# Scores moved behind the turned attention weights, between the first and second pair of key rows, in a one-core attention and channel-mix kernel

## The chip, the cores and the metric

One core of a Trainium2 chip. The metric is the device time of one execution in microseconds (us); the kernel before takes 578.88 us, the median of three runs (578.82 to 579.36). Below, PE is the matrix engine (TensorE), DVE the vector engine, ACT the scalar engine, SP the engine whose queue issues nearly all DMAs.

## The reference

Attention inside chunks of 64 tokens, per batch (8) and head (8), then a channel mix over 512 channels in which each token also sees its predecessor:

```python
scores = q_c @ k_c^T / sqrt(64)              # chunks of 64 tokens, head size 64
attn   = softmax(scores);  x = attn @ v_c     # heads side by side: 8 x 576 x 512
xk = mu_k * x + (1 - mu_k) * x_prev;  xr = mu_r * x + (1 - mu_r) * x_prev
k  = relu(xk @ w_k) ** 2                      # 512 -> 1024
out = sigmoid(xr @ w_r) * (k @ w_v)           # 1024 -> 512
```

All in float32. The large products run as three float32r matmuls over a high and a low part of each operand.

## The kernel before, in words

The 4608 tokens are 18 groups of 256. After a start-up (table `START`), the loop `group(g)` writes one **period** for each of the groups 2 to 17. A period holds the channel mix of group g and the attention of the next groups. Its order is written out by hand in the string `GROUP` (line 56): `K1.0` is step 0 of task `K` with index 1 in this period; a first character is a condition on g from `WHEN` (line 1294); a step that a line names a second time has been issued already and is skipped. Each engine runs its own instructions in the order in which the words stand. In a period PE does:

- `K0` to `K3` (`moe_k`, line 636): four pairs of key rows, 24 matmuls of 256 columns each, into `pk`. ACT takes each out of PSUM (relu, square).
- `Pq.0` (`group_turned`, line 1078): 8 transposes of the normalised attention weights of group g+1 into `pt`, behind `K0`. Step `Pq.1` copies `pt` to SBUF on ACT.
- `R0`, `R1` (`moe_r`, line 689): 24 matmuls of 512 columns into `pr`; ACT's sigmoid (line 703) takes each out.
- `Pq.2` (line 1096): attention times v into `xps`, 32 small products on 64x64 quarters of the array (each shows as two matmuls), then `Nn.0` (`group_scores`, line 1010): the scores of group g+2 into `s`, in the same form. Only the scores read `qT` and `kT`.
- `W` (`moe_halves`, line 909): seven products of 12 matmuls of 256 columns. The first goes to `vx` (called X), the second to `vyz` (called Z). `W.16` is DVE's last step on X, W.3 to W.14 are other steps of DVE and ACT on these results.

On DVE, `De` (`turn`, line 386) turns 256 tokens of q and k from a ring in SBUF into `qT` and `kT`, `Lm` loads the next half ring (32 DMAs on SP), `Lv` loads v for the next products (8 DMAs on SP). `Sn` is the softmax of group g+2 (max, subtract, exp on ACT, sum, reciprocal, normalise = `Sn.6`), `Mr` the mix for `R` (mix on DVE, high part on ACT, low part on DVE).

PSUM is four pools: `ps_s` (one buffer, shared in turn by `s` and `pt`), `ps_x` (one buffer, `xps` and `vyz` in turn), `ps_k` (two, `pk`), `ps_o` (two, `pr` and `vx` in turn). So X waits for the sigmoid of the first `pr`, and Z for ACT's copy of `xps` (line 1122).

Of the kernel before, what the change touches and what calls it, by code (L numbers as in the profile page):

```python
# [7 lines left out]
F32 = mybir.dt.float32  # L8
# [3 lines left out]
AF = mybir.ActivationFunctionType  # L12
# [4 lines left out]
P = 128  # L17
CH = 64
TT = 128
# [34 lines left out]


GROUP = """
=Nc.0 K0.0 =L4 <Sc.0 <Sc.1 K0.12 >Pq.0 >Pq.1 Mr.0 De.01 Lm <Sc.2 K0.3 B.01 K0.4 K1.0 K1.12 E.0 Mr.1 <Sc.3456 Mr.2 K1.34 K2.0 K2.12 E.1 H.0 K2.34 B.23
K3.0 <Pq.0 K3.12 Z.0 <Pq.1 K3.34 Z.1 H.1 H.3 Z.2 H.4 Z.3 H.2 H.5 Z.456
R0.0 R1.0 Pq.2 +Nn.0 Lv Z.78 R0.1 R1.1 Pq.3 Pq.4 C.0 B.4567 C.2 Md.0 Mk.0 B.8 C.4
V0 V1.0 W.0 W.1 W.2 !W.3 !W.4 W.5 W.6 W.7 Mk.1 W.8 W.9 *Sn.0 *Sn.1 W.10 *Sn.2 Mk.2 =Dl.01 C.1 C.3 V1.12345678 C.5 *Sn.3456 W.12 W.11 ~W.3 ~W.4 W.13 W.14 W.15 W.16 =Nn.0  # L60
"""


# [18 lines left out]
def tile_chunk_attention_channel_mix(  # L82
# [12 lines left out]
    nc = tc.nc  # L95
    B_, H, S, D = q.shape
    DM, FF = w_k.shape
    w_k, w_v, w_r = (w.bitcast(I32) for w in (w_k, w_v, w_r))
    HP = H // 2
# [3 lines left out]
    NG = B_ * S // G  # L103
# [19 lines left out]
    ps_s = ctx.enter_context(tc.tile_pool(name="ps_s", bufs=1, space=PSUM))  # L123
    ps_x = ctx.enter_context(tc.tile_pool(name="ps_x", bufs=1, space=PSUM))
    ps_k = ctx.enter_context(tc.tile_pool(name="ps_k", bufs=2, space=PSUM))
    ps_o = ctx.enter_context(tc.tile_pool(name="ps_o", bufs=2, space=PSUM))

    do = Steps()
    T = {}
# [36 lines left out]
    HB = NBLK // 2  # L166
# [96 lines left out]
    B = {}  # L263
# [191 lines left out]
    def x_tile(g):  # L455
        return xp.tile([P, NB, G + 4], F32, tag="x", name=f"x_{g}")
# [527 lines left out]

    def group_scores(g):

        b0, b1 = 8 * g, 8 * g + 8
        late = HB * 4 if g == 4 else b1
        for part, (first, last) in enumerate(((b0, late), (late, b1))):
            do.task = f"D{g}{'el'[part]}"
            for nm in "qk":
                if first < last:
                    do(lambda _, nm=nm, first=first, last=last: turn(nm, first, last - first), "D")

        do.task = f"N{g}"  # L1000

        def f_s(_):
            T[f"s{g}"] = ps_s.tile([P, 2, 2, HP, CH], F32, tag="s", name=f"s_{g}")
            back = -1 if g > SPLIT else 1
            for tl in (0, 1)[::back]:
                for hp in range(HP):
                    for e in (0, 1)[::back]:
                        cols = slice(tl * TT + e * CH, tl * TT + (e + 1) * CH)
                        for j in range(2):
                            nc.tensor.matmul(  # L1010
                                T[f"s{g}"][halves[e], j, tl, hp, :],
                                qT[halves[j], hp, cols],
                                kT[halves[j], hp, cols],
                                start=True,
                                stop=True,
                            )

        do(f_s, "P")

    def load_period(m):  # L1020

        return max(2, (HB * m - 10) // 8 - 2)

    def group_attention(g):
        do.task = f"S{g}c"
# [45 lines left out]
    def group_turned(g):  # L1071
        do.task = f"P{g}q"

        def f_tr(_):
            T[f"pt{g}"] = ps_s.tile([P, 2, HP, TT], F32, tag="s", name=f"pt_{g}")
            for tl in range(2):
                for hp in range(HP):
                    nc.tensor.transpose(  # L1078
                        out=T[f"pt{g}"][:, tl, hp, :],
                        in_=T[f"pg{g}"][:, tl, 2 * hp : 2 * hp + 2, :],  # L1080
                        identity=ident,
                    )

        def f_pT(_):
            T[f"pTg{g}"] = att.tile([P, 2, HP, TT], F32, tag="p", name=f"pT_{g}", bufs=1)
            nc.scalar.activation(T[f"pTg{g}"], T[f"pt{g}"], AF.Copy)

        def f_pv(_):
            T[f"xps{g}"] = ps_x.tile([P, NB, G], F32, tag="x", name=f"xps_{g}")
            for tl in range(2):  # L1090
                for a in range(HP // 2):
                    for e in range(2):
                        for c in range(2):
                            for j in range(2):
                                hp = 2 * a + c
                                nc.tensor.matmul(  # L1096
                                    T[f"xps{g}"][
                                        halves[c], 2 * j + a, tl * TT + e * CH : tl * TT + (e + 1) * CH
                                    ],
                                    T[f"v{2 * g + tl}"][halves[j], hp, e, :],  # L1100
                                    T[f"pTg{g}"][halves[j], tl, hp, halves[e]],
                                    start=True,
                                    stop=True,
                                )

        def f_open(_):
            x = T[f"xg{g}"] = x_tile(g)
            if g * G % S == 0:
                nc.vector.memset(x[:, :, 0:1], 0.0)
            elif g == 3:  # L1110
                seg = x_cuts(2 * g - 1)[-1]
                last = seg[2] + seg[1]
                nc.vector.tensor_copy(out=x[:, :, 0:1], in_=xt[2 * g - 1][:, :, last : last + 1])
            else:
                s, n, c = group_cuts(g - 1)[-1]
                nc.vector.tensor_copy(out=x[:, :, 0:1], in_=T[f"xg{g - 1}"][:, :, c + n : c + n + 1])
            for s, n, c in group_cuts(g)[1:]:
                nc.vector.memset(x[:, :, c : c + 1], 0.0)

        def f_x(_):  # L1120
            for s, n, c in group_cuts(g):
                nc.scalar.activation(
                    T[f"xg{g}"][:, :, c + 1 : c + 1 + n], T[f"xps{g}"][:, :, s : s + n], AF.Copy
                )

        do(f_tr, "P")
        do(f_pT, "A")
        do(f_pv, "P")
        do(f_open, "D")
        do(f_x, "A")  # L1130
# [69 lines left out]
    for t in range(6):  # L1200
# [5 lines left out]
        if t in (1, 3):  # L1206
            g = t // 2
# [12 lines left out]
    with tc.manual_schedule():  # L1220
        for word in START.split():
            name, _, e = word.partition(":")
# [8 lines left out]

    def group(g):
        now = [m for m in range(4, 2 * B_) if load_period(m) == g]
        for m in now:
            load_blocks(f"m{m}", HB * m, HB)
        if g == 2:
            group_scores(3)
            for nm in "qk":
                del do.steps[f"D3e.{'qk'.index(nm)}"]
        if g + 2 < NG:  # L1240
            for t in (2 * g + 4, 2 * g + 5):
                load_v(t)
            group_scores(g + 2)
        for n in {2: (3,), 3: (4,), 4: (5, 6)}.get(g, (g + 2,)):
            if n < NG:
                group_attention(n)
        if g + 1 < NG:
            group_turned(g + 1)
            group_mix(g + 1)
        for fp in range(NF // 2):  # L1250
            moe_k(g, fp)
        for tl in range(2):
            moe_r(g, tl)
        split_weights(g)
        if g < SPLIT:
            for tl in range(2):
                moe_v(g, (tl,))
        else:
            moe_halves(g)
        steps = late | do.take()  # L1260
        late.clear()
        late.update({k: v for k, v in steps.items() if k.startswith(f"M{g + 1}r")})
        for k in late:
            del steps[k]
        names_of = {
            "L4": ["bqm4", "bkm4"],
            "Lm": [f"b{nm}m{m}" for m in now for nm in "qk"],
            "Lv": [f"v{2 * g + 4}", f"v{2 * g + 5}"],
            "De": [f"D{g + 2}e"],
            "Dl": [f"D{g + 2}l"],  # L1270
            "Nc": [f"N{g + 1}"],
            "Nn": [f"N{g + 2}"],
            "Sc": [f"S{g + 1}c"],
            "Sn": [f"S{g + 2}c"],
            "Pq": [f"P{g + 1}q"],
            "Md": [f"M{g + 1}d"],
            "Mk": [f"M{g + 1}k"],
            "Mr": [f"M{g}r"],
        }
        for word in GROUP.split():  # L1280
            when = WHEN.get(word[0])
            if when:
                if not when(g):
                    continue
                word = word[1:]
            task, _, numbers = word.partition(".")
            for name in names_of.get(task, [f"{task[0]}{g}{task[1:]}"]):
                which = [numbers] if task == "W" else numbers
                for i in which or range(NF + 1):
                    if f"{name}.{i}" in steps:  # L1290
                        fn, e = steps.pop(f"{name}.{i}")
                        fn(e)
        assert not steps, steps.keys()
# [1 line left out]
    WHEN = {  # L1295
        "=": lambda g: g == 2,
        "+": lambda g: g > 2,
        "*": lambda g: g >= 4,
        "<": lambda g: g < 5,
        ">": lambda g: g >= 5,  # L1300
        "!": lambda g: g == NG - 1,
# [34 lines left out]
```

## Time and profile before

| what | before |
|---|---|
| time, median of 3 runs | 578.88 us (578.82 to 579.36) |
| the profiled execution's own time | 577.52 us |
| its span, first to last instruction | 575.7 us |
| PE busy | 566.3 us, 98% |
| DVE busy | 460.1 us, 80% |
| ACT busy | 362.4 us, 63% |
| one period, from `K0` to the next `K0` | 29.42 us |

The span is what the trace covers; the time is 1.8 us more, work around the program. The median of the runs is 1.36 us above the profiled execution. A busy PE is not a PE at its peak, since matmuls overlap: the time is read from the distance between starts, which the chain of work gives.

### The profile page before, as it was taken

To read this page: it belongs to the slowest core of one execution; us is meant where nothing else is said; L and a number is where in the kernel's file an instruction comes from. 1 tells how busy PE (TensorE), PEld (TensorE's weight loads), DVE (VectorE), ACT (ScalarE), POOL (GpSimd) and SP (SyncE) were. 2 spreads that over 40 slices of the span, in tenths; PEclk is the share of its full clock that TensorE was granted. 3 is DMA by queue.
4 is the path that set the end of the run, shared out by engine and by line. 5 is a ranking of instruction groups with operands and counts; after the bars stand their busy time and mean duration, and the time that the engine had idled before them with its cause. 6 is when DMAs were issued, how large, how long until landed. Compare 5 with 4: busy or idle time off the path is not lost.

```text
span 575.7 us, 15315 instructions
## 1 busy us (share of the span) xinstructions
PE 566.3 (98%) x6485; PEld 538.5 (94%) x6485; DVE 460.1 (80%) x763; ACT 362.4 (63%) x535; POOL 0.7 (0%) x6
## 2 busy tenths in 40 slices
PE   8899999999999999999999999999999999999997
PEld 7779999999999999999999999999999999999997
DVE  2799898899978969796969696979697969795744
ACT  4898974473747574748484747474747575666461
POOL 0000000000000000000000000000000000000000
PEclk9999999999999999999999999999999999999999
DMA  9997342443544343430233424343433311111011
GB/s 288 207 319 193 97 72 75 94 70 64 107 107 66 88 67 92 65 93 11 63 64 77 86 56 93 66 86 72 89 70 81 73 42 38 38 39 38 1 38 38
DMA packets 184276, 49.25 MB, mean 86 GB/s; under 512 B 169608, under 2 KB 176272, under 8 KB 184208
## 3 DMA queue, kind: packets, MB, share of 16 engines
q1 hardware_dynamic: 183904, 48.01, 37.0%
q8 instruction: 51, 0.84, 0.6%
q10 hardware_dynamic: 304, 0.27, 0.1%
q14 instruction: 17, 0.14, 0.1%
HBM read 38.80 MB, written 9.44 MB: 84 GB/s over the span
## 4 chain that ended last, share of the span: by engine, by line
PE 94%; DMA 2%; DVE 1%; SPq 1%; ACT 1%; issue 0%
PE pk L636 35%; PE pr L689 17%; PE vx L909 15%; PE vyz L909 11%; PE pv L720 6%; PE xps L1096 3%; PE s L1010 2%; DMA wr_st<-in_moe_w_r 2%; PE pt L1078 2%; PE mxk L580 1%; PE mxr L580 1%; SPq L186 1%; PE xps L494 0%; PE s L410 0%; PE pt L474 0%; DVE m L422 0%
## 5 line engine op out<-in xcount | busy, mean ns | idle before, releaser
L636 PE MATMUL pk<-xkhi,wk 128*128 128x256 f32 x1152 | 208.7, 281 | 0.0
L636 PEld LDWEIGHTS pk<-xkhi,wk 128*128 128x128 f32 x1152 | 179.0, 189 | 0.3
L636 PE MATMUL pk<-xklo,wk 128*128 128x256 f32 x576 | 161.3, 280 | 0.0
L636 PEld LDWEIGHTS pk<-xklo,wk 128*128 128x128 f32 x576 | 108.3, 188 | 0.1
L656 ACT ACTIVATE rr<-pk 128x512 f32<-128x512 f32 x60 | 35.8, 597 | 115.2 <-PE pk L636 115.2
L689 PE MATMUL pr<-wr,xrhi 128*128 128x512 f32 x288 | 89.5, 392 | 0.0
L909 PE MATMUL vyz<-b,kk 128*128 128x256 f32 x540 | 68.9, 277 | 0.0
L909 PE MATMUL vx<-b,ks 128*128 128x256 f32 x540 | 68.9, 277 | 0.0
L909 PEld LDWEIGHTS vx<-b,ks 128*128 128x128 f32 x540 | 64.9, 188 | 0.0
L909 PEld LDWEIGHTS vyz<-b,kk 128*128 128x128 f32 x540 | 64.8, 188 | 0.0
L689 PEld LDWEIGHTS pr<-wr,xrhi 128*128 128x128 f32 x288 | 52.8, 188 | 10.1
L689 PE MATMUL pr<-wr,xrlo 128*128 128x512 f32 x144 | 56.1, 389 | 0.0
L855 DVE TENSOR_TENSOR ss<-rr 128x512 f32<-128x512 f32 x15 | 10.4, 693 | 46.0 <-ACT rr L663 46.0
L938 ACT ACTIVATE u<-vx 128x256 f32<-128x256 f32 x30 | 11.5, 384 | 51.5 <-PE vx L909 51.5
L663 ACT ACTIVATE rr<-rr 128x512 f32<-128x512 f32 x60 | 37.9, 632 | 1.9
L747 DVE TENSOR_TENSOR kk<-rr,kk 128x1024 fp32r<-128x1024 f32 x30 | 35.4, 1222 | 2.9 <-ACT kk L893 1.6
L720 PE MATMUL pv<-b,kk 128*128 128x256 f32 x288 | 33.9, 277 | 0.0
L720 PEld LDWEIGHTS pv<-b,kk 128*128 128x128 f32 x288 | 33.1, 188 | 0.1
L689 PEld LDWEIGHTS pr<-wr,xrlo 128*128 128x128 f32 x144 | 27.0, 188 | 5.8
L747 DVE TENSOR_TENSOR xrlo<-mr,xrhi 128x1024 fp32r<-128x1024 f32 x15 | 18.4, 1225 | 15.4 <-ACT xrhi L1168 15.4
L747 DVE TENSOR_TENSOR ks<-ss,ks 128x512 fp32r<-128x512 f32 x45 | 28.3, 684 | 0.0
L1158 DVE SCALAR_TENSOR_TENSOR mk<-d,mu,x 128x256 f32<-128x256 f32 (+3 forms) x80 | 27.7, 413 | 0.4
(130 smaller groups left out, 882.0 us busy)
## 6 DMA issues: line engine op xcount, KB each, us to landing
v<-in_v SPq DMA_DIRECT2D x144, 64.0 KB, 2.4
out<-sg SPq DMA_DIRECT2D x34, 256.0 KB, 2.3
q_ring<-in_q SPq DMA_DIRECT2D x192, 36.0 KB, 2.0
k_ring<-in_k SPq DMA_DIRECT2D x192, 36.0 KB, 2.1
wk_st<-in_moe_w_k SPq DMA_DIRECT2D x4, 1024.0 KB, 11.7
wv_st<-in_moe_w_v SPq DMA_DIRECT2D x4, 1024.0 KB, 7.7
wr_st<-in_moe_w_r SPq DMA_DIRECT2D x2, 1024.0 KB, 10.3
q_ring<-in_q SPq DMA_DIRECT2D x2, 512.0 KB, 6.7
```

What stands on the lines that cost most here:

```text
L580: nc.tensor.matmul(m[:, cb, s : s + w], diag[nm, n][:, cb], x[:, cb, c0 : c0 + w], start=(n == 0), stop=(n == 1),)
L636: nc.tensor.matmul(pk[:, e, :], wk[a][:, cb, f * P : (f + 1) * P], xk[b][:, cb, :], start=(n == 0), stop=(n == 3 * NB - 1),)
L656: nc.scalar.activation(r, T[f"pk{g}{fp}"], AF.Relu)
L663: nc.scalar.activation(r, r, AF.Square)
L689: nc.tensor.matmul(pr, xr[a][:, cb, tl * TT : (tl + 1) * TT], wr[b][:, cb, :], start=(n == 0), stop=(n == 3 * NB - 1),)
L720: nc.tensor.matmul(T[f"pv{g}{tl}"][:, cols[c]], kk[a][:, f, tok[tl]], quarter(f // HF, c)[:, b, f % HF, :], start=(f == 0 and n == 0 and c ...
L747: nc.vector.tensor_tensor(to, x, y, ALU.subtract)
L909: nc.tensor.matmul(to, a[i][:, f, :], weight(w, j, f), start=first and f == 0 and n == 0, stop=f == HF - 1 and n == 2, skip_group_check=True,)
L1010: nc.tensor.matmul(T[f"s{g}"][halves[e], j, tl, hp, :], qT[halves[j], hp, cols], kT[halves[j], hp, cols], start=True, stop=True,)
L1078: nc.tensor.transpose(out=T[f"pt{g}"][:, tl, hp, :], in_=T[f"pg{g}"][:, tl, 2 * hp : 2 * hp + 2, :], identity=ident,)
L1096: nc.tensor.matmul(T[f"xps{g}"][halves[c], 2 * j + a, tl * TT + e * CH : tl * TT + (e + 1) * CH], T[f"v{2 * g + tl}"][halves[j], hp, e, :] ...
L1158: nc.vector.scalar_tensor_tensor(out=to[:, cb, s : s + w], in0=T[f"d{g}"][:, cb, s : s + w], scalar=mu[:, cb : cb + 1], in1=T[f"xg{g}"][:, ...
```

## The change

For the scores of group n, formed in period n-2:

- Periods 6 to 15: the scores stand directly behind the transposes `Pq.0`, between `K0` and `K1`. In period 5 they stand between `K2` and `K3`. In periods 2 to 4 nothing changes.
- From period 5 on, `pt` is two tiles in `ps_o` and no longer one in `ps_s`. The copy `pT` on ACT becomes two instructions of 128x512 (in all periods).
- q and k are turned three periods ahead and not two, from group 8 on (`turn_period`). Period 5 turns groups 7 and 8, and loads two half rings. `De` stands ahead of `Mr.0` from period 5 on.
- On DVE, `W.16` (X taken out) moves ahead of the normalising step `Sn.6` in periods 4 to 16. The products on PE keep their order.

```diff
-=Nc.0 K0.0 =L4 <Sc.0 <Sc.1 K0.12 >Pq.0 >Pq.1 Mr.0 De.01 Lm <Sc.2 K0.3 B.01 K0.4 K1.0 K1.12 E.0 Mr.1 ...
+=Nc.0 K0.0 >Pq.0 $Nn.0 =L4 <Sc.0 <Sc.1 K0.12 >Pq.1 >De.01 Mr.0 De.01 #K1.0 #K2.0 #Nn.0 ^Lm <Sc.2 K0.3 B.01 K0.4 K1.0 K1.12 E.0 Mr.1 <Sc.3456 Mr.2 #D8.01 #Lm K1.34 ...
-R0.0 R1.0 Pq.2 +Nn.0 Lv ...
+R0.0 R1.0 Pq.2 %Nn.0 Lv ...
-... C.5 *Sn.3456 W.12 W.11 ~W.3 ~W.4 W.13 W.14 W.15 W.16 =Nn.0
+... C.5 *Sn.345 W.12 W.15 *W.16 *Sn.6 W.11 ~W.3 ~W.4 W.13 W.14 W.16 =Nn.0
...
-        return max(2, (HB * m - 10) // 8 - 2)
+        return max(2, turn_period((HB * m - 10) // 8))
+    def turn_period(g):
+        return g - 2 if g < 8 else g - 3
...
-            T[f"pt{g}"] = ps_s.tile([P, 2, HP, TT], F32, tag="s", name=f"pt_{g}")
+            if g < 6:
+                x = ps_s.tile([P, 2, HP, TT], F32, tag="s", name=f"pt_{g}")
+                T[f"pt{g}"] = [x[:, tl] for tl in range(2)]
+            else:
+                T[f"pt{g}"] = [ps_o.tile([P, HP, TT], F32, tag="o", name=f"pt{tl}_{g}") for tl in range(2)]
...
-            nc.scalar.activation(T[f"pTg{g}"], T[f"pt{g}"], AF.Copy)
+            for tl in range(2):
+                nc.scalar.activation(T[f"pTg{g}"][:, tl], T[f"pt{g}"][tl], AF.Copy)
...
-            "De": [f"D{g + 2}e"],
+            "De": [f"D{g + 2 if g < 6 else g + 3}e"],
+            "D8": ["D8e"],
...
-        "*": lambda g: g >= 4,
+        "*": lambda g: 4 <= g < NG - 1,
+        "%": lambda g: 3 <= g < 5,
+        "#": lambda g: g == 5,
+        "^": lambda g: g != 5,
+        "$": lambda g: g >= 6,
```

PE in period 8, before: the last matmul of `K0`, the transposes, the first of `K1`; further on the last of `R1`, `xps`, the scores of group 10, and the first of X.

```order
L636 MATMUL pk_8_0_3990<-xkhi_8_3871,wk1_119 128x256
L1078 MATMUL pt_9_4018<-ident_109,p_9_3948 128x128 x8
L636 MATMUL pk_8_1_4070<-xkhi_8_3871,wk0_118 128x256
...
L689 MATMUL pr_8_1_4186<-wr0_120,xrlo_8_4030 128x512
L1096 MATMUL xps_9_4199<-pT_9_4027,v_18_3850 64x64 x16
L1096 MATMUL xps_9_4199<-pT_9_4027,v_19_3855 64x64 x16
L1010 MATMUL s_10_4232<-kT_123,qT_122 64x64 x32
L909 MATMUL vx_8_4293<-b11_978,kk0_8_4126 128x256 x2
```

The same places of the changed kernel:

```order
L636 MATMUL pk_8_0_4033<-xkhi_8_3914,wk1_119 128x256
L1085 MATMUL pt0_9_4058<-ident_109,p_9_3991 128x128 x4
L1085 MATMUL pt1_9_4059<-ident_109,p_9_3991 128x128 x4
L1007 MATMUL s_10_4068<-kT_123,qT_122 64x64 x32
L636 MATMUL pk_8_1_4150<-xkhi_8_3914,wk0_118 128x256
...
L689 MATMUL pr_8_1_4266<-wr0_120,xrlo_8_4112 128x512
L1104 MATMUL xps_9_4279<-pT_9_4104,v_18_3893 64x64 x16
L1104 MATMUL xps_9_4279<-pT_9_4104,v_19_3898 64x64 x16
L909 MATMUL vx_8_4340<-b11_978,kk0_8_4206 128x256 x2
```

One run of 64x64 work in a period has become two, and X stands directly behind `xps`.

DVE at the turn from period 8 to 9, before: the softmax sums of group 10 (`z`), the normalising step, six steps on the products of group 8, then the mix `mr`, the turn of q and k, and the low part of `xr`.

```order
L1057 RECIPROCAL z_10_4368<-z_10_4368 128x16
L1061 TENSOR_TENSOR p_10_4363<-p_10_4363,z_10_4368 128x1024
L952 TENSOR_TENSOR sg_8_1_4279<-u1_8_4308,sg_8_1_4279 128x256
...
L952 TENSOR_TENSOR sg_8_0_4277<-vx_8_4293,sg_8_0_4277 128x256
L1158 SCALAR_TENSOR_TENSOR mr_9_4446<-d_9_4284,mu2_115,x_9_4281 128x256 x4
L386 STREAM_TRANSPOSE qT_122<-q_ring_116 128x4x64
...
L747 TENSOR_TENSOR xrlo_9_4445<-mr_9_4446,xrhi_9_4444 128x1024
```

And in the changed kernel:

```order
L1058 RECIPROCAL z_10_4415<-z_10_4415 128x16
L952 TENSOR_TENSOR sg_8_0_4324<-vx_8_4340,sg_8_0_4324 128x256
L1062 TENSOR_TENSOR p_10_4410<-p_10_4410,z_10_4415 128x1024
L952 TENSOR_TENSOR sg_8_1_4326<-u1_8_4355,sg_8_1_4326 128x256
...
L386 STREAM_TRANSPOSE qT_122<-q_ring_116 128x1024
L386 STREAM_TRANSPOSE kT_123<-k_ring_117 128x1024
L1166 SCALAR_TENSOR_TENSOR mr_9_4530<-d_9_4331,mu2_115,x_9_4328 128x256 x4
L747 TENSOR_TENSOR xrlo_9_4529<-mr_9_4530,xrhi_9_4528 128x1024
```

The step on `vx` has moved ahead of the normalising step, and the turns ahead of `mr`; they now also wait for the scores of the same period.

SP in periods 5 and 6 of the changed kernel:

```order
L223 DMA q_ring_116<-in_q 32x9x32 x16
L223 DMA k_ring_117<-in_k 32x9x32 x16
L223 DMA q_ring_116<-in_q 32x9x32 x16
L223 DMA k_ring_117<-in_k 32x9x32 x16
L201 DMA v_14_3080<-in_v 64x4x64 x4
L201 DMA v_15_3085<-in_v 64x4x64 x4
L958 DMA out_0<-sg_5_0_3092 128x512
L958 DMA out_0<-sg_5_1_3094 128x512
```

Before, one q and one k line stood there, and the second pair followed in period 6, behind the stores of group 5.

## Rows read from the trace of the kernel before

**Rows 1.** The page's part 1 (busy time and share of the span; PE and its weight loads) and the granted TensorE clock of part 2, in tenths, in 40 equal slices.

```profile
PE 566.3 (98%) x6485; PEld 538.5 (94%) x6485; DVE 460.1 (80%) x763; ACT 362.4 (63%) x535; POOL 0.7 (0%) x6
PEclk9999999999999999999999999999999999999999
```

**Rows 2.** The waits of PE, the longest in total: line, what released it, total us, times, longest.

```profile
PE s L410 <- DVE p L430: 1.5, 1, 1.5
```

**Rows 3.** The chain of work that ended last, period 9: start us, us, engine, tile, line, count. A piece counts up to the end of its last matmul, so its duration is the distance from the end before.

```profile
311.37 2.83 PE pk L636 x24
314.20 0.87 PE pt L1078 x8
315.08 8.48 PE pk L636 x72
323.56 5.47 PE pr L689 x24
329.03 1.09 PE xps L1096 x64
330.12 0.93 PE s L1010 x64
331.05 1.57 PE vx L909 x12
332.62 1.36 PE vyz L909 x12
...
340.79 2.83 PE pk L636 x24
```

**Rows 4.** The same chain, period 16, in which no scores are left to form, and the start of period 17 (no scores, no transposes).

```profile
534.92 1.09 PE xps L1096 x64
536.01 0.03 issue
536.04 1.63 PE vx L909 x12
537.67 1.47 PE vyz L909 x12
539.14 1.41 PE vx L909 x12
...
546.20 10.90 PE pk L636 x96
```

**Rows 5.** The same chain in the start-up and in period 2: scores (s) between other work, and what follows them.

```profile
53.19 0.62 PE s L410 x32
53.81 8.38 PE pk L636 x72
62.19 5.46 PE pr L689 x24
67.66 8.48 PE pk L636 x72
...
103.31 1.09 PE s L1010 x64
104.40 11.08 PE pk L636 x96
```

**Rows 6.** ACT in order of time, periods 8 and 16 (start us, duration us): relu of `K3` (line 656), the two sigmoids (703), the copy of `xps` (1122).

```profile
294.19 0.60 ACT L656 ACTIVATE rr<-pk 128x512 f32<-128x512 f32 x1 [1.04 <-PE pk L636]
300.08 1.09 ACT L703 ACTIVATE sg<-pr 128x512 f32<-128x512 f32 x2
301.05 1.04 ACT L1122 ACTIVATE x<-xps 128x1024 f32<-128x1024 f32 x1
...
529.49 0.60 ACT L656 ACTIVATE rr<-pk 128x512 f32<-128x512 f32 x1 [1.05 <-PE pk L636]
535.39 1.09 ACT L703 ACTIVATE sg<-pr 128x512 f32<-128x512 f32 x2
536.36 1.04 ACT L1122 ACTIVATE x<-xps 128x1024 f32<-128x1024 f32 x1
```

**Rows 7.** DVE in order of time, the start of period 8 (its `K0` starts at 281.80): normalising step, the step on `vx`, the mix, the turn of q, the low part of `xr`.

```profile
282.56 1.23 DVE L1061 TENSOR_TENSOR p<-p,z 128x1024 f32<-128x1024 f32 x1
...
285.62 0.42 DVE L952 TENSOR_TENSOR sg<-vx,sg 128x256 f32<-128x256 f32 x1
285.95 1.66 DVE L1158 SCALAR_TENSOR_TENSOR mr<-d,mu,x 128x256 f32<-128x256 f32 x4
287.54 1.24 DVE L386 STREAM_TRANSPOSE qT<-q_ring 128x1024 f32<-128x1024 f32 x1
...
290.77 1.23 DVE L747 TENSOR_TENSOR xrlo<-mr,xrhi 128x1024 fp32r<-128x1024 f32 x1 [0.88 <-ACT xrhi L1168]
```

**Rows 8.** SP in order of time, period 5 (its `K0` starts at 193.56), and from the page's part 6 the median us from issue to landing.

```profile
200.56 8.84 SPq L223 DMA_DIRECT2D q_ring<-in_q  x16
209.51 8.68 SPq L223 DMA_DIRECT2D k_ring<-in_k  x16
218.29 5.25 SPq L201 DMA_DIRECT2D v<-in_v  x8
226.94 0.84 SPq L958 DMA_DIRECT2D out<-sg  x2
...
v<-in_v SPq DMA_DIRECT2D x144, 64.0 KB, 2.4
out<-sg SPq DMA_DIRECT2D x34, 256.0 KB, 2.3
```

More of the change, by code (lines that the diff above doesn't have):

```diff
@@ L56 @@
 GROUP = """
-=Nc.0 K0.0 =L4 <Sc.0 <Sc.1 K0.12 >Pq.0 >Pq.1 Mr.0 De.01 Lm <Sc.2 K0.3 B.01 K0.4 K1.0 K1.12 E.0 Mr.1 <Sc.3456 Mr.2 K1.34 K2.0 K2.12 E.1 H.0 K2.34 B.23
+=Nc.0 K0.0 >Pq.0 $Nn.0 =L4 <Sc.0 <Sc.1 K0.12 >Pq.1 >De.01 Mr.0 De.01 #K1.0 #K2.0 #Nn.0 ^Lm <Sc.2 K0.3 B.01 K0.4 K1.0 K1.12 E.0 Mr.1 <Sc.3456 Mr.2 #D8.01 #Lm K1.34 K2.0 K2.12 E.1 H.0 K2.34 B.23
 K3.0 <Pq.0 K3.12 Z.0 <Pq.1 K3.34 Z.1 H.1 H.3 Z.2 H.4 Z.3 H.2 H.5 Z.456
-R0.0 R1.0 Pq.2 +Nn.0 Lv Z.78 R0.1 R1.1 Pq.3 Pq.4 C.0 B.4567 C.2 Md.0 Mk.0 B.8 C.4
-V0 V1.0 W.0 W.1 W.2 !W.3 !W.4 W.5 W.6 W.7 Mk.1 W.8 W.9 *Sn.0 *Sn.1 W.10 *Sn.2 Mk.2 =Dl.01 C.1 C.3 V1.12345678 C.5 *Sn.3456 W.12 W.11 ~W.3 ~W.4 W.13 W.14 W.15 W.16 =Nn.0
+R0.0 R1.0 Pq.2 %Nn.0 Lv Z.78 R0.1 R1.1 Pq.3 Pq.4 C.0 B.4567 C.2 Md.0 Mk.0 B.8 C.4
+V0 V1.0 W.0 W.1 W.2 !W.3 !W.4 W.5 W.6 W.7 Mk.1 W.8 W.9 *Sn.0 *Sn.1 W.10 *Sn.2 Mk.2 =Dl.01 C.1 C.3 V1.12345678 C.5 *Sn.345 W.12 W.15 *W.16 *Sn.6 W.11 ~W.3 ~W.4 W.13 W.14 W.16 =Nn.0
 """
@@ L982, in moe_halves, with group_turns @@
         do(scale(0, 1, X), "D")
-    def group_scores(g):
+    def group_turns(g):
         b0, b1 = 8 * g, 8 * g + 8
@@ L998, in group_scores @@
                     do(lambda _, nm=nm, first=first, last=last: turn(nm, first, last - first), "D")
+    def group_scores(g):
         do.task = f"N{g}"
@@ L1074, in f_tr @@
         def f_tr(_):
-            T[f"pt{g}"] = ps_s.tile([P, 2, HP, TT], F32, tag="s", name=f"pt_{g}")
+            if g < 6:
+                x = ps_s.tile([P, 2, HP, TT], F32, tag="s", name=f"pt_{g}")
+                T[f"pt{g}"] = [x[:, tl] for tl in range(2)]
+            else:
+                T[f"pt{g}"] = [
+                    ps_o.tile([P, HP, TT], F32, tag="o", name=f"pt{tl}_{g}") for tl in range(2)
+                ]
             for tl in range(2):
@@ L1078, in f_tr @@
                     nc.tensor.transpose(
-                        out=T[f"pt{g}"][:, tl, hp, :],
+                        out=T[f"pt{g}"][tl][:, hp, :],
                         in_=T[f"pg{g}"][:, tl, 2 * hp : 2 * hp + 2, :],
@@ L1237, in group @@
             group_scores(3)
-            for nm in "qk":
-                del do.steps[f"D3e.{'qk'.index(nm)}"]
         if g + 2 < NG:
@@ L1243, in group @@
             group_scores(g + 2)
+        for n in range(4, NG):
+            if turn_period(n) == g:
+                group_turns(n)
         for n in {2: (3,), 3: (4,), 4: (5, 6)}.get(g, (g + 2,)):
```

## The prediction

> **What bounds the kernel now.** I read the page's part 1 first, then the waits of PE, then the chain, and the other engines last. Part 1 shows PE busy for 98% of the span, with the granted clock at 9 tenths or more in every slice [rows 1]. That alone proves little, because matmuls overlap. The waits decide: the longest wait of PE is 1.5 us, once, in the start-up [rows 2]; every other one in that list is in the start-up too. So from period 3 on nothing that DVE, ACT or a DMA does sets the end, and the time is the length of PE's own stream. A period is 29.42 us (311.37 to 340.79) [rows 3]. Work hidden behind PE earns nothing; an edit counts only if it changes the distance between PE's instructions or brings a wait.
>
> Two things set those distances.
>
> First, **a run of 64x64 products costs more when it stands alone.** `xps` takes 1.09 us and `s` directly behind it 0.93 [rows 3], but `s` by itself takes 1.09 [rows 5]. So the entry costs 0.16 us, and one run in place of two pays it once. The exit costs as well: the first product behind the run takes 1.57 us and its like 1.36 [rows 3], so 0.21. The transposes use the whole array and cost 0.87 with no visible entry [rows 3].
>
> Second, **the 256-column matmuls run at one of two paces.** `pk` in a usual period takes 8.48 us for 72, or 0.118 each; in period 17 it takes 10.90 for 96, or 0.1135 [rows 3, 4]. W products take 1.36 or 1.41 for 12, the same two paces. What comes before decides: behind a run of 64x64 the pace is the quick one (8.38 for 72 with the exit in it, 11.08 for 96) [rows 5]; behind `pr` or the transposes it is the slow one (8.48) [rows 3, 5]; from quick W into `K0` it turns slow (2.83 for 24) [rows 3]. In period 16 it turns slow inside W, where Z starts late (1.47, then 1.41), and the next `K` is quick [rows 4]. I have no cause for this and use it as seen.
>
> **The change part by part.** Period 16 is the template for what is left behind `xps`: it has no scores, so X stands directly behind it, as it will in periods 5 to 15.
>
> *The scores.* At their new place they stand alone: 1.09 for 0.93, so +0.16. `K1` to `K3` then run behind a 64x64 run: 8.38 for 8.48, so -0.10.
>
> The Trainium skill, page "TensorE: Matmul & The Clock Gate", section "Step-by-step: what each phase is for", says that PE loads weights ahead of running matmuls, so that by it a second run would cost no entry and the sum below would be about 1.8 us smaller. The page "TensorEngine Tiling (Array Packing)", section "Key Properties", speaks against the change: switching the tiling mode drains the engine. The rows side with the second (1.09 against 0.93), and I keep the measured term.
>
> *X and Z.* Before, 0.93 us of scores lay between `xps` and X. ACT's chain from the relu of `K3` to the sigmoid takes 5.9 us in period 8 (294.19 to 300.08) and in period 16 (529.49 to 535.39) alike [rows 6]. It starts from `K3`, and `K3` now ends about a microsecond later in the period while X does not: the cover of the sigmoid, and of the copy of `xps` behind it (1.04), is gone. In period 16 that gave X a wait and 1.63 for 1.57 (+0.09 with the 0.03 of issue ahead of it), Z 1.47 for 1.36 (+0.11) and the five products behind Z 1.41 for 1.36 (+0.25) [rows 4]. I take all three. Between "no wait at all" (0) and these (+0.45), period 16 is the nearer row: same instructions, same order on ACT.
>
> *`K0` of the next period* is then quick: 10.90/96 x 24 = 2.73 for 2.83, so -0.10 [rows 3, 4].
>
> A period gains 0.16 - 0.10 + 0.09 + 0.11 + 0.25 - 0.10 = +0.41; ten periods (6 to 15) give +4.1.
>
> *Period 5* has the scores between `K2` and `K3`. 48 matmuls at the slow pace are 5.65, the 24 behind the scores 8.38 - 48 x 0.1135 = 2.93, together 8.58 for 8.48: +0.10. With +0.16 and the +0.45 of X and Z: +0.71. *Period 16* gains only a quick `K0`: -0.10. The sum is +4.7.
>
> *Edits that I cost at nothing.* The step on `vx` ahead of the normalising step delays the latter by 0.33 (285.62 to 285.95). It ended at 283.79, 2.0 into the period, and the transposes start at 2.83 (2.73 with the quick `K0`): the margin falls from 0.8 to 0.4 [rows 3, 7]. Without it the transposes wait, 1 us for 1 us. The second `pt` tile takes X's buffer, free by the same step. The turns now wait for the scores, which end 4.7 into the period, where DVE arrives at 4.2: a wait of some 0.6. Behind it stand the two turns (2.4), `mr` (1.6), on ACT the high part (1.0), then the low part (1.2), so that `xrlo` is there at about 11.4; `pr` starts at 2.73 + 0.87 + 1.09 + 8.38 = 13.1. Cover 1.7, where it was 2.0 [rows 3, 7]. The copy `pT` in two pieces costs ACT a few tenths, in its gap ahead of the relu of `K1`.
>
> *SP in period 5* is where a queue moves: 64 ring loads stand ahead of v and the stores. They start some 1.6 us sooner (the turns no longer follow `mr`), at 199.0, and at 8.84 and 8.68 per 16 they end near 234.5; v ends near 239.7 and has landed by 241.6; the first store is issued at 239.8 and lands near 242.3 [rows 8]. Period 6 starts near 223.7, needs v at 242.2, and the store's buffer for its sigmoid near 242.9. It fits by 0.6 us, so I take 0, with up to 1.5 as the upper bound for slower issue.
>
> The profiled execution took 577.52, so the sum gives 582.2 for one like it. The median of the runs is 1.36 above it; I forecast **583.6**.
>
> **The rivals.**
> - *Cover holds:* X and Z find the sigmoid and the copy done, W keeps 1.36 and `K0` 2.83. A period then gains +0.16 - 0.10 = +0.06, period 5 +0.26: +0.9, so 579.8. For: X begins only 0.03 late in period 16 [rows 4]. Against: the 5.9 us of ACT leave no slack. 0.13.
> - *Wait without the slow pace:* X +0.09, Z +0.06, the rest at 1.36, `K0` at 2.83: +0.21 a period, +0.41 in period 5, so +2.5 and 581.4. For: one period alone shows the pace turn. 0.11.
> - *All quick (the other side):* two 64x64 runs a period put every 256-column stream at the quick pace, `K0` too, and the entry behind the transposes is free, since both are plain float32: -0.10 - 0.10 a period, so -2.0 and 576.9. It decides at X: if the sigmoid is done 0.1 us sooner than in period 16. Against: 53.19 shows scores behind float32 work paying the entry (0.62 for 32 [rows 5], where half of 0.93 is 0.47), and `K0` is slow behind quick W in every period of rows 3. 0.06.
> - *SP is late:* were all 64 loads to take 10 us per 16, v would land 5 us later and period 6 would wait some 4 us: 587.6. For: nothing was queued so long before. Against: both rows of period 5 are under 9 [rows 8]. 0.04.
>
> **How the numbers follow.** The forecast has 0.66. Its own range is 582.3 to 585.6: below, if the pace turns back halfway; above, if `K0` stays slow (+1.0) or SP costs a microsecond. The whole range reaches down to the covered case, 579.6, and up to 586.0; that leaves out the quick case and SP in full. A measurement tells about 0.2%, or 1.2 us, from no change. Slower by more: 0.66 + 0.11 + 0.04 = 0.81; within: 0.13; faster: 0.06.
>
> **What would show it.** In the chain of a period from 6 to 15: `s` at 1.09 behind `pt`, `pk` x72 at 8.38, X near 1.63 with a small issue ahead of it, Z near 1.47, five products at 1.41, `K0` near 2.73, the period 29.83. In the waits of PE nothing from DVE at `pt`, nothing from a DMA at `xps`. I am wrong if W stays at 1.36 (cover holds), if `K0` stays at 2.83 behind a slow W, or if a period is shorter than 29.42.

## The result, and the profile after

The changed kernel takes **585.83 us** (median of 6 runs, 583.58 to 587.65) against 578.85 (6 runs, 577.22 to 579.63): a ratio of 1.0123, 95% interval 1.0093 to 1.0153. It is slower by 7.0 us where 4.7 were forecast: above the forecast's own range, which ended at 585.6, and just inside the whole range, which ended at 586.0.

Executions of both kernels differ by some 2 us in the start-up (in the profiled ones period 4 begins at 164.31 before and at 166.64 after, with a granted clock of 1.00 and 0.91 between 20 and 40 us), and two single executions of the runs below, of 707.71 and 1993.38 us, are left out, so what follows compares pieces of the chain from period 5 on and not spans.

Part 1 of the page after and the granted clock of part 2, which answer to [rows 1]:

```profile
PE 575.3 (98%) x6485; PEld 543.8 (93%) x6485; DVE 458.8 (78%) x763; ACT 363.9 (62%) x550; POOL 0.7 (0%) x6
PEclk9899999999999999999999999999999999999999
```

PE does the same 6485 instructions and is busy 9.0 us longer, at the same share of the span; the one slice at 8 lies in the start-up. The longest wait of PE is still the one of [rows 2]. Nothing in a list of waits tells where 7 us went. The chain does: period 5, period 8 with the start of 9, and the end of 9 (start us, us, engine, tile, line, count), which answer to [rows 3, 4].

```profile
199.76 5.65 PE pk L636 x48
205.41 1.09 PE s L1007 x64
206.50 3.03 PE pk L636 x24
...
286.43 2.74 PE pk L636 x24
289.17 0.87 PE pt L1085 x8
290.04 1.09 PE s L1007 x64
291.14 8.68 PE pk L636 x72
299.81 5.47 PE pr L689 x24
305.28 1.09 PE xps L1104 x64
306.37 0.03 issue
306.40 1.65 PE vx L909 x12
308.06 1.44 PE vyz L909 x12
309.50 1.41 PE vx L909 x12
...
316.57 2.74 PE pk L636 x24
...
336.54 1.65 PE vx L909 x12
338.19 1.40 PE vyz L909 x12
339.58 1.36 PE vx L909 x12
...
346.38 2.83 PE pk L636 x24
```

Period 8 is 30.14 long (286.43 to 316.57), where a period was 29.42 [rows 3]. Piece by piece against [rows 3]: scores +0.16, `K1` to `K3` **+0.20** (8.68 for 8.48), X +0.11 with its issue, Z +0.08, five products +0.26, `K0` -0.09: +0.72. In period 9 the products behind Z stay at 1.36 and the next `K0` at 2.83, which makes +0.51. Periods 6 to 15 are 30.03 in the mean (226.34 to 526.62), or +0.61 each; period 5 is 30.29 (+0.87), and period 16 is 28.55 for 28.94.

ACT in period 8, which answers to [rows 6]: relu of `K3`, the sigmoids, the copy of `xps`.

```profile
299.85 0.60 ACT L656 ACTIVATE rr<-pk 128x512 f32<-128x512 f32 x1 [1.05 <-PE pk L636]
...
305.75 1.08 ACT L703 ACTIVATE sg<-pr 128x512 f32<-128x512 f32 x2
306.72 1.04 ACT L1130 ACTIVATE x<-xps 128x1024 f32<-128x1024 f32 x1
```

From the relu to the sigmoid it is 5.90 us, as before [rows 6]; X is due at 306.37, when `xps` ends, 6.52 after the relu began, and the first of the two sigmoids ends in the middle of its 1.08. So X begins 0.03 late, and Z follows the copy. Of the 5.90, 1.28 is the load of ACT's function table for the sigmoid, which begins at 304.46. And DVE there, which answers to [rows 7]: the turn of q, the low part of `xr`.

```profile
291.20 1.35 DVE L386 STREAM_TRANSPOSE qT<-q_ring 128x256 f32<-128x256 f32 x2 [0.99 <-PE s L1007]
...
296.44 1.23 DVE L747 TENSOR_TENSOR xrlo<-mr,xrhi 128x1024 fp32r<-128x1024 f32 x1 [1.14 <-ACT xrhi L1176]
```

DVE waits 0.99 for the scores, and `xrlo` ends at 297.67, 2.1 ahead of `pr` (299.81). No edit that was costed at nothing shows on the chain.

### The profile page after: what moved, and what is told of

It reads as the page before. It is cut to its first block, busy times and chain, and to the rows that moved or that the text cites. A ratio compares the mean times of both kernels' runs of the same rounds, so it can differ in the third digit from the quotient of the medians.

```text
span 584.8 us, 15333 instructions
## 1 busy us (share of the span) xinstructions
PE 575.3 (98%) x6485; PEld 543.8 (93%) x6485; DVE 458.8 (78%) x763; ACT 363.9 (62%) x550; POOL 0.7 (0%) x6
## 4 chain that ended last, share of the span: by engine, by line
PE 96%; DVE 2%; ACT 1%; issue 0%; ACTq 0%
PE pk L636 35%; PE pr L689 16%; PE vx L909 15%; PE vyz L909 11%; PE pv L720 6%; PE s L1007 3%; PE xps L1104 3%; PE pt L1085 2%; PE warm L1233 1%; PE trq L367 1%; PE trk L367 1%; PE s L410 1%; PE mxk L580 1%; PE mxr L580 1%; PE pt L474 0%; PE xps L494 0%
## 5 line engine op out<-in xcount | busy, mean ns | idle before, releaser
L909 PE MATMUL vyz<-b,kk 128*128 128x256 f32 x540 | 70.1, 279 | 0.0
L938 ACT ACTIVATE u<-vx 128x256 f32<-128x256 f32 x30 | 11.5, 384 | 43.3 <-PE vx L909 43.3
```

Of the source, the lines that this page charges most:

```text
L909: nc.tensor.matmul(to, a[i][:, f, :], weight(w, j, f), start=first and f == 0 and n == 0, stop=f == HF - 1 and n == 2, skip_group_check=True,)
```

## The experiments

The question is which part of +0.61 a period belongs to the place of the scores, which to the lost cover of the sigmoid, and whether the buffers and DVE's order have a part. Each ratio is to runs of the kernel before on the same chip.

| run | ratio, 95% | a period |
|---|---|---|
| scores put back | 0.9987 [0.9971, 1.0003] | 29.42 |
| sigmoid's chain shorter | 1.0096 [1.0076, 1.0115] | 29.7 to 29.8, or 30.2 |
| scores ahead of `K0` | 1.0096 [1.0072, 1.0121] | 29.8 to 30.2, once 30.72 |
| both, transposes behind `K3` | 1.0046 [1.0026, 1.0066] | 29.36, or 29.8 to 29.9, once 30.90 |
| the same, second wait gone | 1.0018 [1.0002, 1.0034] | 29.36, once 31.51 |
| sigmoid's chain shorter, second wait gone | 1.0085 [1.0062, 1.0108] | 29.77, once 30.88 |
| scores ahead of the transposes | one execution | 29.5 to 29.9, once 30.29 |
| scores between `K1` and `K2` | one execution | 29.8 to 30.3, once 34.22 |
| fifth run, second half ring later | 0.9997 [0.9982, 1.0013] | 29.36 |
| scores ahead of the transposes, no waits | 1.0007 [0.9989, 1.0025] | 29.41 |

The last column is for periods 6 to 15; each "once" is period 6, in which ACT waits for a store, as shown below.

**Scores put back**, with the turns; the two `pt` tiles, the copy in two pieces and the early step on `vx` stay.

```diff
-K0.0 >Pq.0 $Nn.0 ... K0.12 >Pq.1 >De.01 Mr.0 De.01 #K1.0 #K2.0 #Nn.0 ^Lm ... #D8.01 #Lm
+K0.0 >Pq.0 ... K0.12 >Pq.1 Mr.0 De.01 Lm ...
-        "%": lambda g: 3 <= g < 5,
+        "%": lambda g: g > 2,
```

> The changed kernel with its scores and its turns of q and k back at their old places; the two pt tiles in ps_o, the copy pT in two pieces and W.16 ahead of the normalising step stay. Theory (the place of the scores makes all of it): the chain is that of the kernel before, s 0.93 behind xps, X 1.57, Z 1.36, period 29.42, time 578.9 (within 1.2). Rival (the buffers or the moved DVE steps delay PE): X or the transposes wait, the period stays above 29.6 and the time above 581.

577.48 us (577.16 to 579.4), where the kernel before beside it took 579.15; the interval of the ratio holds 1. The chain is that of [rows 3]:

```profile
403.18 8.48 PE pk L636 x72
...
417.13 1.09 PE xps L1104 x64
418.22 0.93 PE s L1007 x64
419.15 1.57 PE vx L909 x12
420.72 1.36 PE vyz L909 x12
```

The buffers, the copy in two pieces and the early step on `vx` cost nothing. All of it hangs on where the scores stand, with the turns and loads that go with that place.

**Sigmoid's chain shorter.** The last of ACT's steps between the relu of `K3` and the sigmoid leaves that place: `H.5` (line 896, 0.64 us), part of the operand sums of the products, and with it DVE's `Z.8`, which uses it, follow the copy of `xps` (`Pq.4`).

```diff
-... H.2 H.5 Z.456
-R0.0 R1.0 Pq.2 %Nn.0 Lv Z.78 R0.1 R1.1 Pq.3 Pq.4 C.0 ...
+... H.2 <H.5 Z.456
+R0.0 R1.0 Pq.2 %Nn.0 Lv Z.7 <Z.8 R0.1 R1.1 Pq.3 Pq.4 >H.5 >Z.8 C.0 ...
```

> The changed kernel; on ACT the last high part of W's sums (H.5) and on DVE its low part (Z.8) stand behind the copy of xps, so that both sigmoids and that copy start 0.63 us sooner. Theory (X and Z wait for ACT, and the wait throws W's pace): no issue ahead of X, X 1.57, Z 1.36, W at 1.36 in every period, K0 at 2.83, K1 to K3 still 8.69; period 29.77, 0.26 less than 30.03 in the mean, time about 2.9 below the changed kernel, 583.0. Rival (what X and Z lose is the exit of a run that follows pr directly): X 1.65 and Z 1.40 to 1.50 as before, time 585.8.

584.22 us (583.43 to 586.23), 1.2 over the expectation. Two pieces of its chain:

```profile
424.96 0.69 DVE ks L747
425.66 1.21 DVE d L747 x2
426.86 2.12 DVE mk L1166 x8
...
429.00 1.06 ACT xkhi L1176
...
430.38 1.64 PE vyz L909 x12
...
452.39 1.09 PE xps L1104 x64
453.49 1.57 PE vx L909 x12
455.06 1.36 PE vyz L909 x12
```

At 452 the theory holds to the hundredth: no issue, X 1.57, the rest 1.36, `K0` 2.83, the period 29.77. At 424 the moved step has made a wait of its own. Where a batch ends inside the 256 tokens the mix `mk` comes in eight pieces and not four; `Z.8` now stands ahead of it, and waits for ACT's `H.5`. So the mix is late, then ACT with the high part of `xk` (`xkhi`), and a product further back in W waits for ACT to take out an earlier one. These are the periods of 30.2; they are called cut periods below. That was my edit, not the change's. (In period 6 it also waited for a store, told below.)

**Scores ahead of `K0`.**

```diff
-=Nc.0 K0.0 >Pq.0 $Nn.0 =L4 ...
+=Nc.0 $Nn.0 K0.0 >Pq.0 =L4 ...
```

> The changed kernel with the scores one step sooner, between the last W product and K0; the transposes stay between K0 and K1. Theory (a 64x64 run sets the quick pace unless work at the slow pace or the transposes stood ahead of it): K0 behind the scores at 0.1135 each plus the exit, about 2.83, K1 to K3 behind the transposes at 8.48; period about 29.97. Rival (the pace behind a run is always the slow one in these periods): K0 2.95. Both give 585.0 to 586.0; the chain tells them apart.

584.55 us (583.56 to 587.05).

```profile
317.29 1.09 PE s L1007 x64
318.38 2.94 PE pk L636 x24
...
322.20 8.48 PE pk L636 x72
```

`K1` to `K3` are back at 8.48. For `K0` I had expected 2.83 and left the exit out: the quick pace with its exit is 24 x 0.1135 + 0.21 = 2.93, so 2.94 is quick, while the changed kernel's last pair of period 5 (3.03) is the slow pace with its exit. The rival's 2.95 was too low as well, so by the numbers as they were expected this run alone doesn't decide; the next one does, with 96 matmuls in place of 24. X stays late by 0.03, since nothing was done for ACT.

**Both, with the transposes behind `K3`**: the scores ahead of `K0` and the sooner sigmoid of the second run together, and `pt` in the buffer of `xps`. The 96 matmuls of `K` follow the scores in one row.

```diff
-=Nc.0 K0.0 >Pq.0 $Nn.0 =L4 ... K0.12 >Pq.1 >De.01 ...
-K3.0 <Pq.0 K3.12 Z.0 <Pq.1 ...
+=Nc.0 $Nn.0 K0.0 =L4 ... K0.12 >De.01 ...
+K3.0 Pq.0 K3.12 Z.0 Pq.1 ...
```

> The changed kernel with the scores ahead of K0, the transposes behind K3 (pt in ps_x, which xps takes over), and the sooner sigmoid. Theory (pace as in the row of 104.40, waits gone): pk x96 in 11.08 behind s 1.09, pt 0.87, pr 5.47 to 5.56, X 1.57, Z and the rest 1.36; period 29.34, time 578 to 579, 7 us below the changed kernel. Rival 1 (K slow behind scores in any case): pk x96 11.5, period 29.77, 583. Rival 2 (the copy pT, now between relu and sigmoid on ACT, delays X): X late by up to 1 us, period above 30, 587 or more.

581.34 us (580.13 to 585.3), 2.3 over the upper end of the expectation. The quick pace came, here in period 13:

```profile
433.57 1.09 PE s L1007 x64
434.66 11.10 PE pk L636 x96
```

At the slow pace with its exit these 96 would take some 11.5. Periods that are not cut take 29.36. Cut ones stay at 29.82 to 29.86 by the same wait as in the second run, and period 6 waits for a store.

**The second wait gone.** `Z.8` goes behind the mix `Mk.0` in the last run, and likewise in the second.

```diff
-... Pq.4 >H.5 >Z.8 C.0 B.4567 C.2 Md.0 Mk.0 B.8 C.4
+... Pq.4 >H.5 C.0 B.4567 C.2 Md.0 Mk.0 >Z.8 B.8 C.4
```

> The run with the scores ahead of K0, the transposes behind K3 and the sigmoid of the second half sooner, with one more move: DVE's step on that half's sum (Z.8) stands behind the last mix of the next input and no longer ahead of it. Theory (all that kept its periods 6 to 15 from 29.35 us was the chain copy of xps, sum on ACT, Z.8, mix, high part, W, in the periods whose tokens a batch boundary cuts): Z goes back to 1.36 in all of them, every period is 29.35 for 29.42 of the kernel before, the ten periods give -0.7, and with periods 5, 16 and 17 near those of before the time is 577 to 579, within 0.3% of the kernel before. Rival (the second wait has another releaser): cut periods stay at 29.8, some 2 us in all, and the time is 580 to 582.

> The run with the sigmoid of the second half sooner, and Z.8 behind the last mix; scores and transposes where the changed kernel has them. Theory: X 1.57, Z 1.36, W 1.36, K0 2.83 in every period 6 to 15, a period 29.77 (the place of the scores alone: +0.16 of entry, +0.20 of exit at the slow pace of K1 to K3), and 583 or a little under. Rival (the wait of X in itself costs nothing and the pace evens out): no less than the 585 of the changed kernel; second rival (the second wait has another releaser): cut periods stay at 30.2, 584.

The first gives 579.98 (577.79 to 581.66), some 1 us over its expectation, the other 583.52 (582.33 to 584.38). The periods from 8 to 15 are as expected (29.36 and 29.77): the second wait is settled. The place of the scores alone costs 0.35 a period, the wait at X and Z the other 0.26. In period 6 something else shows. The first one's chain there:

```profile
226.78 11.12 PE pk L636 x96
...
243.02 2.31 DMA out<-sg
...
246.69 0.60 ACT sg L703
...
247.34 1.66 PE vx L909 x12
```

The store of group 5 has stood behind 64 ring loads and v on SP; it is issued at 243.02, and the sigmoid, which reuses its buffer, waits 2.54 for it. This is a mild form of the forecast's rival "SP is late": its loads take 8.65 to 9.32 per 16, not 10, and what comes late is the store, not v. In the profiled execution of the changed kernel the store is issued at 241.89 and lands at 244.32, and ACT is ready for the sigmoid at 244.34: it fits by 0.02, and whether other executions waited isn't shown. Here ACT is ready 1.5 sooner, at 242.86, and the store is issued 1.1 later. The two runs in which the scores stand ahead of `K0` or ahead of the transposes, with ACT's order as in the changed kernel, wait 0.61 and 0.75 there. So a cost that the changed kernel only just escapes comes to light when the others go.

**The second half ring later**, in the run just shown: its 32 loads stand behind the stores of period 5.

```diff
-... W.13 W.14 W.16 =Nn.0
+... W.13 W.14 W.16 =Nn.0 #Ln
-            "Lm": [f"b{nm}m{m}" for m in now for nm in "qk"],
+            "Lm": [f"b{nm}m{m}" for m in (now[:1] if g == 5 else now) for nm in "qk"],
+            "Ln": [f"b{nm}m{m}" for m in now[1:] for nm in "qk"],
```

> The run with the scores ahead of K0, the transposes behind K3 and both waits gone, with one more move: the 32 loads of the second half ring that period 5 put ahead of v and the stores on SP follow the stores of period 5, as in the kernel before. In the run without this move, stores issued at 243.0 landed 2.3 later, and the sigmoid of period 6 waited for them; period 6 was 31.51 for 29.36. Theory (SP's queue of period 5 is all of that): stores are issued near 227, period 6 goes to 29.36, 2.1 us less than in the run without the move; against the kernel before, 0.06 less in each of periods 6 to 15, 0.4 less in period 16, 0.3 more in period 5, so 0.7 in all, a ratio of 0.999. Rival (period 6 waits for another load, or the second half ring now comes late for period 7): period 6 or 7 stays 1 to 2 us longer, ratio 1.002.

577.36 us, the kernel before 577.67. Period 6 is 29.37, so the queue is shown. The 0.7 that I had worked out did not come: the ten periods give -0.5, period 16 -0.5 and period 5 +0.35 as expected, but period 17, which I had left out, gives +0.4 (`K` at 11.31 for 10.90), and from period 5 to the end it is 381.8 for 382.0. That is below what a measurement tells.

**Scores between `K1` and `K2`**, and **scores ahead of the transposes**, one execution of each: what is it that leaves `K1` to `K3` slow?

```diff
-K0.0 >Pq.0 $Nn.0 =L4 ...
+K0.0 >Pq.0 $K1.0 $Nn.0 =L4 ...
```

> The changed kernel with the scores between K1 and K2 in periods 6 to 15, the transposes still behind K0. If it is the transposes directly ahead of the scores that leave K1 to K3 at the slow pace: K1 slow behind the transposes (2.83), scores 1.09, K2 and K3 quick behind them, 48 x 0.1135 + 0.21 = 5.66, sum of K1 to K3 8.49. If any 64x64 run inside a row of key products leaves it at the pace it had or at the slow one: K2 and K3 48 x 0.118 + 0.20 = 5.86, sum 8.69, as in the changed kernel (8.68).

```profile
291.81 2.83 PE pk L636 x24
294.64 1.09 PE s L1007 x64
295.73 5.85 PE pk L636 x48
```

588.52 us, with a wait for the store in period 6 (34.22 long). Slow again, without transposes directly ahead: the first idea falls. (The turns stand behind `mr` here, a second difference, which leaves these pieces of PE alone.)

```diff
-K0.0 >Pq.0 $Nn.0 =L4 ...
+K0.0 $Nn.0 >Pq.0 =L4 ...
```

> The changed kernel with the scores ahead of the transposes, both between K0 and K1, in periods 6 to 15. By the rows: scores behind K0 1.09; the transposes behind a 64x64 run, 0.87 plus an exit of 0.1 to 0.2; K1 to K3 behind the transposes 8.48. If the exit is paid by whatever comes next, the sum from K0's end to K3's is 10.54 to 10.64 (changed kernel 0.87 + 1.09 + 8.68 = 10.64), so a period no longer, and up to 0.1 shorter. If the transposes take no exit, 10.44, a period 0.2 shorter than in the changed kernel.

```profile
285.37 2.83 PE pk L636 x24
288.20 1.09 PE s L1007 x64
289.29 1.02 PE pt L1085 x8
290.31 8.18 PE pk L636 x72
```

582.43 us, and neither of my two cases: the transposes take 0.15 of exit, and `K1` to `K3` behind them are **quick**, 8.18 or 0.1136 each. The four pieces are 13.12, where before `K0`, `pt`, `K1` to `K3` and `s` were 13.11. In this order the new place costs PE nothing.

**Scores ahead of the transposes, no waits**: that order, the second run's sigmoid with `Z.8` behind `Mk.0`, and the later half ring.

> The changed kernel with the scores ahead of the transposes, both between K0 and K1, with the sigmoid of the second half sooner and Z.8 behind the last mix (no wait at X or Z), and with the second half ring's loads behind the stores of period 5. Theory (the changed kernel pays the order of scores and transposes, the wait of X and the queue of period 5, and nothing else): K0 2.83, scores 1.09, transposes 1.02, K1 to K3 8.18, pr 5.47, xps 1.09, X 1.57, six products of 1.36, a period 29.41, as before (29.42), and a time within 0.2% of the kernel before. Rival (scores between pairs of key rows cost 0.35 a period in whatever order): a period of 29.75 to 29.8 and a ratio of 1.006.

577.88 us (577.63 to 580.09), ratio 1.0007. The period is 29.41 (282.40 to 311.81):

```profile
282.40 2.83 PE pk L636 x24
285.23 1.09 PE s L1007 x64
286.32 1.02 PE pt L1085 x8
287.35 8.18 PE pk L636 x72
...
302.08 1.57 PE vx L909 x12
```

Three things taken back, the order of scores and transposes, the wait at X and the queue of period 5, and the scores may stand between the key rows for the price they had.

## Why the prediction was right, and where it was not

- **The bound.** Right: PE's own stream sets the time, and the two prices of the change, a second entry into 64x64 work and the lost cover of the sigmoid, are what the runs show. The entry is 1.09 for 0.93 in every run in which scores stand alone.
- **The step that failed**: "`K1` to `K3` then run behind a 64x64 run: 8.38 for 8.48, so -0.10". They took 8.68, so +0.20, in each of the ten periods: 3.0 us. I had taken two rows of the start-up and of period 2 [rows 5] for a rule on what comes before. In both of them other work stood ahead of the scores (`mxk`, line 580, and `pv`, line 720); the kernel before has no row with scores behind the transposes `pt` and ahead of key products, or inside a row of key products. The rule doesn't hold there: transposes then scores, or `K1` then scores, leave the stream slow; scores then transposes, or the last W product then scores, leave it quick.
- **X and Z.** Right in kind and size: in periods 5 to 15 0.03 or 0.04 of issue, X 1.64 to 1.66, Z 1.40 to 1.51, and "cover holds" fell. The second run shows the wait itself: with the sigmoid sooner X is 1.57 and Z 1.36.
- **The five products behind Z at 1.41**: half right. Slow in periods 5, 7, 8, 10 and 15, quick in the other six of 5 to 15, and `K0` is the other way round (2.74 or 2.83), as forecast. That W stays at 1.36 was the prediction's own sign of being wrong, and the six periods are its rival "wait without the slow pace", which had a chance of 0.11. Period 16 of before, one row, was one of two outcomes: with the scores put back the same order of PE's work gives X 1.68, Z 1.38 and the rest at 1.36 there, the period 28.64 for 28.94. The six quick periods came out some 0.17 below the forecast's terms, about -1.0 in all.
- **Luck.** These -1.0 hid part of the first miss of +3.0, so the ten periods gave +6.1 for +4.1; with period 5 (+0.87 for +0.71), period 16 (-0.39 for -0.10) and 17 with the end (+0.1) the sum is +6.7 for +4.7. The rest to 7.0 lies within the spread of the start-ups. The time stayed inside the whole range by 0.2 us; without the second error, of the opposite sign, it would have been some 586.8.
- **Costed at nothing**: the transposes, `xrlo`, the copies and the store of period 5 show no wait in the profiled execution of the changed kernel. The terms given for `xrlo` add up to 10.9 and not 11.4; measured, it was 2.1 ahead of `pr`. The 0.6 us that I gave SP were 0.02 there, and with the sigmoid due sooner and the store later PE stood for 2.1 us in another run.
- **All quick**, the rival that ended faster, has the right mechanism in the wrong arrangement: two lone runs can put `K` at the quick pace, but a period is then shorter by 0.06 only, and only without a wait at X.
- The drain at a switch of modes ("TensorEngine Tiling (Array Packing)", section "Key Properties", in the Trainium skill) agrees with what every run here shows: 0.16 in and 0.15 to 0.21 out. No run shows the drain itself. The entry was paid in every run, so the sum that the prediction set beside its own, smaller by 1.8, did not come.

**Open**: why a stream of 256-column matmuls runs at 0.1135 or 0.118. It isn't the clock: in the changed kernel it is granted in full (1.00, so 2.4 GHz) from 309.5 to 316.5, where products take 1.41, and from 339.6 to 346.3, where they take 1.36. Open with it: why the order of scores and transposes sets the pace of the key products behind.

## What to carry to other kernels

When PE never waits, moving work on it is not free: price the switch into and out of 64x64 work, and what the moved piece had covered on another engine (here 0.93 us of scores over 5.9 us of ACT). Put such a run where its neighbours were measured, not where one row elsewhere suggests a pace: swapping it with the eight transposes was worth 0.36 us a period. And a queue that fits by half a microsecond is a cost waiting for the next improvement.

## What the runs showed of the hardware

The 256-column matmuls have two steady paces at a full clock, and which one comes after a stall of hundredths of a microsecond is not settled by the length of the stall at Z. There are 53 places in the two kernels and the ten runs where X began behind the sigmoid with such a stall. Sorted by the time of X and Z together, the products behind were quick at 3.04 to 3.08 us (24 times), slow at 3.09 to 3.10 (13), quick at 3.11 to 3.12 (8) and slow at 3.15 to 3.16 (8), without an exception. This sum is no measure of the stall, though: a Z at the slow pace is itself 0.05 longer. The stall at Z shows in the trace's records of single matmuls as the distance from its first matmul to its second. That distance is 149 ns with quick products behind (the run with the scores between `K1` and `K2`, X at 398.01) and 149 ns with slow ones (the run with the scores ahead of `K0`, X at 307.13). A few hundredths of a microsecond thus go with 0.05 us in each of the five products behind, and what decides is not shown.
